# Decay attention with a softplus FFN: score halves of the later units summed out of PSUM by one reduction, masked once, then split; the low parts of k and q on VectorE

## The chip, the core and the metric

The kernel runs on one core of one Trainium2 chip. The metric is device microseconds of one execution. The median of three runs of the kernel before is 705.5 us (703.51 to 705.92).

Five engines matter here: TensorE (PE in the profile; its weight loads are listed apart as PEld), VectorE (DVE), ScalarE (ACT), GpSimd (POOL), and SyncE (SP), which issues nearly all DMAs. In this program each engine works off one queue, whose order is fixed at compile time, and semaphores tie the queues together; an instruction that waits holds up those behind it in its queue.

## The reference

```python
def _attn_ref(q, k, v):                      # (4, 8, 768, 64) each
    gamma = 1.0 - 2.0 ** (-5.0 - np.arange(H))
    scale = 1.0 / np.sqrt(D)
    state = zeros((B, H, D, D))
    for t in range(S):
        state = gamma * state + k_t (outer) v_t
        y[:, :, t] = scale * q_t @ state

def _moe_ref(x, w_in, w_out):                # x: 3072 x 512, w_in: 512 x 2048, w_out: 2048 x 512
    h = x @ w_in
    g = np.maximum(h, 0.0) + np.log1p(np.exp(-np.abs(h)))
    return g @ w_out
```

The attention's result, with heads side by side, is the x of the second function. All is float32, and the weights arrive as float64. The kernel gets its precision by splitting float32 numbers into a high part (rounded to fp32r) and a low part (the rest), and by running three matmuls for one product: high x high, high x low, low x high.

## The kernel before

**Units.** The attention runs in chunks of C = 128 tokens. A unit is one batch, one chunk and four of the eight heads (`HH = 4`, as `NJ = 2` pairs): 4 x 6 x 2 = 48 units. Every unit goes through the same parts at fixed ticks (L302: `load_unit` at -6, `decay` at -2, `operands` at 0, `scores` at 2, `new_state` at 3, `stack_and_outputs` at 5), and units follow each other every 4 ticks.

**Early and later units.** The first `WHOLE = 12` units use whole float32 matmuls. The 36 later ones use split operands:

- `load_unit` (L141) loads kn (keys by tokens, for the state), then kb and qb (keys and queries in 32-wide blocks; `load_blocks`, L131, 8 DMAs of 16 KB each, issued at L136), then vn (values by tokens), all on SP's queue. kn, kb and the pair qn/qb have two buffers each. kn is loaded for every unit, though the last chunk of a batch makes no state and never reads it. vn goes into the first of two halves of three fixed tiles `vns`; the other half is zero and serves only the early units.
- `decay` (L156) multiplies qb (L166) and vn (L167) by tables, on POOL.
- `operands` (L169): DVE transposes kb and qb in place (L185); ACT copies k's high part (L189) and q's (L192, L193); POOL subtracts for the low parts of k (L190) and of q (L194), two 64x256 instructions each. Then the split of v into `vhl` (L197 on ACT, L198 on DVE).
- `scores` (L201): for each pair j, two matmuls (L215) put into one PSUM tile `sc` two fields beside each other: field 0 is (k high and low) x q high, field 1 is that x q low. ACT copies field 0 into the high part `ah` (L217); DVE subtracts `ah` from field 0 (L218) and adds field 1 (L219), which makes `al`. After both pairs, POOL masks `ah` and `al` (L221, two instructions of 128x512).
- `new_state` (L228): the state matmuls of kn and vn (L238). `outputs` (L262): matmuls of q with the state (L287, L288), of `vhl` with `ah` and `al` (L289 to L291), then the split of the result into the ring `xh`, `xl` (L293 on ACT, L295 on DVE). `stack_state` (L246) splits the state (L258 on ACT, L260 on DVE).

**FFN.** It runs over nine blocks of tokens (`BLOCKS`: 256, 256, six of 384, 256) in steps of one or two of the sixteen 128-wide slices of `DF`. A step is `hidden` (L316, matmuls L323 to L325 out of the ring into `hp`, two PSUM buffers), `softplus_1` (L328: L330 on DVE, L331 on ACT), `softplus_2` (L333: L335 on DVE, high part gh L337 on ACT, low part gl L339 on POOL) and, two steps later, `second` (L342, L354 to L356), at whose end the results are copied out (`o`, two buffers; L366, L368) and stored (L370, on SP).

**Order.** The code spreads the ticks over the FFN's steps, so that a block's units are done about two steps ahead of it; a compile-time simulation of the engines then fixes the order on every queue. The weights (L70, L71) are loaded and converted (L78 to L99) in the first 100 us, each load paced by an earlier conversion.

Of the kernel before, what the change touches and what calls it, by code (L numbers as in the profile page):

```python
# [10 lines left out]
F32 = mybir.dt.float32  # L11
F32R = mybir.dt.float32r
# [3 lines left out]
ALU = mybir.AluOpType  # L16

P = 128
C = 128
# [6 lines left out]
WHOLE = 12  # L26
# [7 lines left out]
def decay_attention_then_softplus_ffn(ctx: ExitStack, tc: tile.TileContext, q, k, v, w_in, w_out, qtab, vtab, gtab, out):  # L34
    nc = tc.nc
    B, H, S, D = q.shape
    DM, DF = w_in.shape
    NC = S // C
# [5 lines left out]
    HH = H // 2  # L44
    NJ = HH // 2

    const = ctx.enter_context(tc.tile_pool(name="const", bufs=1))
    attn = ctx.enter_context(tc.tile_pool(name="attn", bufs=1))
# [53 lines left out]
    units = [(c // NC, c % NC, hf) for c in range(B * NC) for hf in range(2)]  # L102
    loads, live, state = {}, {}, {}
# [20 lines left out]
    vns = [attn.tile([P, HH, 2, D], F32, name=f"vn{i}") for i in range(3)]  # L124
# [4 lines left out]


    def load_blocks(nm, src, b, c, hf):  # L131
        t = attn.tile([P, NJ, C // 32, 32], F32, name=nm, tag={"qb": "qn"}.get(nm, nm), bufs=2)
        for h in range(HH):
            for d in range(0, D, 32):
                at = h % 2 * D + d
                nc.sync.dma_start(  # L136
                    t[at:at + 32, h // 2], src[b, hf * HH + h, c * C:(c + 1) * C, d:d + 32].rearrange("(i t) d -> t i d", t=32)
                )
        return t

    def load_unit(n):  # L141
        if n in loads:
            return
        b, c, hf = units[n]
        tiles = []
        for nm, src in (("kn", k), ("qn", q), ("vn", v)):
            if nm == "qn" and n >= WHOLE:
                for nm, src in (("kb", k), ("qb", q)):
                    tiles.append(load_blocks(nm, src, *units[n]))
                continue  # L150
            t = vns[n % 3][:, :, 0, :] if nm == "vn" else attn.tile([P, HH, D], F32, name=nm, bufs=2)
            nc.sync.dma_start(t, src[b, hf * HH:(hf + 1) * HH, c * C:(c + 1) * C, :].rearrange("h s d -> s h d"))
            tiles.append(t)
        loads[n] = tiles

    def decay(n):  # L156
        b, c, hf = units[n]
        vn = loads[n][-1]
        hs = slice(hf * HH, (hf + 1) * HH)
        if n < WHOLE:  # L160
            qn = loads[n][1]
            nc.gpsimd.tensor_tensor(qn, qn, qtabs[:, c, hs].unsqueeze(2).broadcast_to([P, HH, D]), op=ALU.mult)
        else:
            qb = loads[n][2].rearrange("p m i d -> p (m i) d")
            by = qblocks[:, c, hf].rearrange("p m i -> p (m i)")
            nc.gpsimd.tensor_tensor(qb, qb, by.unsqueeze(2).broadcast_to(list(qb.shape)), op=ALU.mult)  # L166
        nc.gpsimd.tensor_tensor(vn, vn, vtabs[:, c, hs].unsqueeze(2).broadcast_to([P, HH, D]), op=ALU.mult)  # L167

    def operands(n):  # L169
        b, c, hf = units[n]  # L170
        kn, *rest, vn = loads.pop(n)
        if n < WHOLE:
            tp = ps_a.tile([P, 2, NJ, C], F32, name="tp", tag="a")
            for t, x in enumerate((kn, *rest)):
                for j in range(NJ):
                    nc.tensor.transpose(tp[:, t, j, :], x[:, 2 * j:2 * j + 2, :], ident)
            qt = qs[:, n % 2]
            nc.scalar.copy(kz[lo, 0], tp[lo, 0])
            nc.vector.tensor_copy(kz[up, 1], tp[up, 0])
            nc.scalar.copy(qt, tp[:, 1])  # L180
            live[n] = [qt, kn, vn]
            return
        for x in rest:
            blocks = x.rearrange("p m i d -> p (m i d)")
            nc.vector.transpose(blocks, blocks)  # L185
        kt, qt = (x.rearrange("p m i d -> p m (i d)") for x in rest)
        kq = kqs[n % 2]
        for par, own, oth in sides:
            nc.scalar.copy(kq[own, 0, par], kt[own])  # L189
            nc.gpsimd.tensor_tensor(kq[oth, 0, par], kt[own], kq[own, 0, par].bitcast(F32), op=ALU.subtract)  # L190
        for par, own, oth in sides:
            nc.scalar.copy(kq[own, 1, par], qt[own])  # L192
            nc.scalar.copy(kq[oth, 1, par], qt[own])  # L193
            nc.gpsimd.tensor_tensor(kq[own, 2, par], qt[own], kq[own, 1, par].bitcast(F32), op=ALU.subtract)  # L194

        vhl = attn.tile([P, HH, 2, D], F32R, name="vhl", tag="vhl", bufs=2)
        nc.scalar.copy(vhl[:, :, 0, :], vn)  # L197
        nc.vector.tensor_tensor(vhl[:, :, 1, :], vn, vhl[:, :, 0, :].bitcast(F32), op=ALU.subtract)  # L198
        live[n] = [kq, vhl, kn, vn]

    def scores(n):  # L201
        kq = live[n][0]
        if n < WHOLE:
            parts = [attn.tile([P, HH, C], F32, name="ah")]
            sc = ps_a.tile([P, HH, C], F32, name="sc", tag="a")
            for h in range(HH):
                nc.tensor.matmul(sc[:, h, :], lhsT=kz[:, h % 2, h // 2, :], rhs=kq[:, h // 2, :], start=True, stop=True)
            nc.scalar.copy(parts[0], sc)
        else:
            parts = [attn.tile([P, HH, C], F32R, name=nm) for nm in ("ah", "al")]  # L210
            for j in range(NJ):

                sc = ps_a.tile([P, 2, 2, C], F32, name="sc", tag="a")
                for par in range(2):
                    nc.tensor.matmul(sc[:, par], lhsT=kq[:, 0, par, j, :], rhs=kq[:, 1:, par, j, :], start=True, stop=True)  # L215
                hi, low = (t[:, 2 * j:2 * j + 2, :] for t in parts)
                nc.scalar.copy(hi, sc[:, :, 0, :])  # L217
                nc.vector.tensor_tensor(low, sc[:, :, 0, :], hi.bitcast(F32), op=ALU.subtract)  # L218
                nc.vector.tensor_tensor(low, sc[:, :, 1, :], low.bitcast(F32), op=ALU.add)  # L219
        for t in parts:  # L220
            nc.gpsimd.affine_select(  # L221
                t, t.bitcast(F32), pattern=[[0, HH], [1, C]], compare_op=ALU.is_ge, fill=0.0, base=0, channel_multiplier=-1
            )
        live[n] += parts

    began = {}

# [72 lines left out]


    PARTS = {-6: load_unit, -2: decay, 0: operands, 2: scores, 3: new_state, 5: stack_and_outputs}  # L302
    FIRST_TICK = min(PARTS)
    PERIOD = 4
# [72 lines left out]
    for i, a, b in turns:  # L377
        m = WIDE // BLOCKS[i]
# [18 lines left out]
    for n in range(2):  # L397
        load_unit(n)
# [44 lines left out]
    for a, b in zip(starts, starts[1:]):  # L443
        i = steps[b][0]
        if i == 2:
            a = b - SPREAD
        have = ticks_for(i - 1)
        for s in range(a, b):

            t, n = (s - a + 1, b - a) if i == 2 else (min(s - a, b - a - 2), b - a - 2)  # L450
# [59 lines left out]
```

## Time and profile before

| | before |
|---|---|
| median of 3 runs | 705.5 us (703.51 to 705.92) |
| profiled execution | 702.99 us, span of its instructions 701.3 us |
| mean granted TensorE clock | 0.988 |
| PE busy | 666.4 us (95%), 4136 matmuls |
| DVE busy | 357.5 us (51%), 771 instructions |
| ACT busy | 362.5 us (52%), 844 |
| POOL busy | 387.6 us (55%), 498 |

A busy time is the union of an engine's instructions. In a list of groups, a line gives the code line, engine, operation, output and inputs, the shape and the count; behind the bar stand the total busy time in us and the mean of one in ns, and then the engine's idle time just before such instructions, with what ended it. In a timeline, the first two numbers are start and duration in us, and a bracket gives idle time before the instruction and what ended it. A stretch of the run shows its length, the busy time of PE, PEld, DVE, ACT and POOL (with instruction counts), the granted TensorE clock as a share of full speed, the share of DMA time and GB/s.

### The profile page before, as it was taken

The page shows a single profiled execution, that of the slowest core. Times are in us where ns is not written, and L with a number is a line of the kernel's source. Part 1 is how long each engine was busy: PE and PEld are TensorE (multiplying, and loading weights), DVE is VectorE, ACT ScalarE, POOL GpSimd, SP SyncE. Part 2 cuts the span into 40 slices and gives each one's busy share as a digit, 9 for nine tenths or more (in the row PEclk, how much of TensorE's full clock was granted, in tenths as well). Part 3 has the DMA queues.
Part 4 walks back from the last instruction along what each step waited for, and adds up shares of the span by engine and source line. Part 5 has one row for each costly group of instructions (what it writes and reads, how often), then busy time and mean ns, then how long its engine had stood idle before and what let it go on. Part 6 is the DMA issues. An engine that isn't in the chain of part 4 may idle for free.

```text
span 701.3 us, 13055 instructions
## 1 busy us (share of the span) xinstructions
PE 666.4 (95%) x4136; PEld 604.0 (86%) x4136; DVE 357.5 (51%) x771; ACT 362.5 (52%) x844; POOL 387.6 (55%) x498
## 2 busy tenths in 40 slices
PE   5888999999999899997999999999899999999997
PEld 4778999988999789986999979998699988999996
DVE  5757877356544554444555446444644446443321
ACT  5767776445445554454555555454555456432221
POOL 5877778545556465554655565556556556322221
PEclk9998999999999999998999999999999999999999
DMA  8889752132121331113212232121221212000100
GB/s 250 216 215 244 204 158 39 33 80 62 32 37 33 87 66 26 34 38 76 39 33 37 46 87 55 26 46 32 72 51 33 36 43 65 1 1 1 46 0 31
DMA packets 156997, 47.57 MB, mean 68 GB/s; under 512 B 143616, under 2 KB 151808, under 8 KB 156928
## 3 DMA queue, kind: packets, MB, share of 16 engines
q1 hardware_dynamic: 156480, 46.72, 28.1%
q8 instruction: 33, 0.54, 0.3%
q14 instruction: 36, 0.29, 0.1%
q10 hardware_dynamic: 448, 0.01, 0.0%
HBM read 40.39 MB, written 6.29 MB: 67 GB/s over the span
## 4 chain that ended last, share of the span: by engine, by line
PE 77%; DMA 5%; POOL 4%; ACT 3%; issue 3%; SPq 3%; DVE 2%; POOLq 0%; ACTq 0%; DVEq 0%
PE hp L323 11%; PE hp L324 11%; PE hp L325 11%; PE acc L355 11%; PE acc L354 11%; PE acc L356 11%; SPq L136 2%; PE sc L215 2%; PE stp L238 2%; DMA win<-in_moe_w_in_dram 1%; POOL kq L190 1%; PE yp L290 1%; PE yp L291 1%; PE yp L289 1%; POOL kq L194 1%
## 5 line engine op out<-in xcount | busy, mean ns | idle before, releaser
L339 POOL TENSOR_TENSOR gl<-sp,gh 128x384 fp32r<-128x384 f32 (+1 forms) x120 | 129.4, 1080 | 180.8 <-ACT gh L337 156.6
L323 PE MATMUL hp<-xh,winhl 128*128 128x384 f32 (+1 forms) x576 | 186.8, 327 | 3.4 <-ACT xh L293 1.7
L324 PE MATMUL hp<-xl,winhl 128*128 128x384 f32 (+1 forms) x576 | 185.6, 322 | 0.0
L325 PE MATMUL hp<-xh,winhl 128*128 128x384 f32 (+1 forms) x576 | 185.5, 322 | 0.0
L354 PE MATMUL acc<-wouthl,gh 128*128 128x512 f32 x384 | 152.9, 398 | 0.0
L355 PE MATMUL acc<-wouthl,gh 128*128 128x512 f32 x384 | 152.1, 396 | 0.0
L356 PE MATMUL acc<-wouthl,gl 128*128 128x512 f32 x384 | 148.5, 395 | 0.1
L331 ACT ACTIVATE sp<-sp 128x384 f32<-128x384 f32 (+1 forms) x120 | 65.5, 546 | 135.6 <-DVE sp L330 129.3
L330 DVE TENSOR_SCALAR sp<-hp 128x384 uint32<-128x384 uint32 (+1 forms) x120 | 69.4, 579 | 107.4 <-PE hp L325 103.3
L323 PEld LDWEIGHTS hp<-xh,winhl 128*128 128x128 f32 x576 | 109.4, 191 | 8.6 <-ACT xh L293 2.0
L324 PEld LDWEIGHTS hp<-xl,winhl 128*128 128x128 f32 x576 | 109.9, 191 | 3.4
L325 PEld LDWEIGHTS hp<-xh,winhl 128*128 128x128 f32 x576 | 109.7, 190 | 0.4
L337 ACT CAST gh<-sp 128x384 fp32r<-128x384 f32 (+1 forms) x120 | 64.1, 535 | 78.3 <-DVE sp L335 40.1
L335 DVE SCALAR_TENSOR_TENSOR sp<-hp,sp 128x384 f32<-128x384 f32 (+1 forms) x120 | 69.5, 579 | 42.9 <-ACT sp L331 41.7
L356 PEld LDWEIGHTS acc<-wouthl,gl 128*128 128x128 f32 x384 | 71.7, 188 | 14.8 <-POOL gl L339 0.5
L354 PEld LDWEIGHTS acc<-wouthl,gh 128*128 128x128 f32 x384 | 72.5, 189 | 11.2
L355 PEld LDWEIGHTS acc<-wouthl,gh 128*128 128x128 f32 x384 | 72.6, 189 | 11.0
L194 POOL TENSOR_TENSOR kq<-qb,kq 64x256 fp32r<-64x256 f32 x72 | 52.8, 733 | 31.9 <-ACT kq L192 24.6
L190 POOL TENSOR_TENSOR kq<-kb,kq 64x256 fp32r<-64x256 f32 x72 | 53.0, 736 | 25.4 <-ACT kq L189 20.6
L185 DVE STREAM_TRANSPOSE kb<-kb 128x256 f32<-128x256 f32 x36 | 16.0, 444 | 66.9 <-DMA kb<-in_k_dram 40.0
L192 ACT CAST kq<-qb 64x256 fp32r<-64x256 f32 x72 | 29.0, 403 | 33.2 <-PE yp L287 26.7
L295 DVE TENSOR_TENSOR xl<-yp,xh 64x256 fp32r<-64x256 f32 x72 | 30.0, 417 | 22.7 <-ACT xh L293 21.8
(80 smaller groups left out, 1010.5 us busy)
## 6 DMA issues: line engine op xcount, KB each, us to landing
win<-in_moe_w_in_dram SPq DMA_DIRECT2D x16, 512.0 KB, 4.5
wout<-in_moe_w_out_dram SPq DMA_DIRECT2D x16, 512.0 KB, 4.2
kn<-in_k_dram SPq DMA_DIRECT2D x48, 128.0 KB, 2.3
vn<-in_v_dram SPq DMA_DIRECT2D x48, 128.0 KB, 2.6
out_dram<-o SPq DMA_DIRECT2D x24, 256.0 KB, 2.1
kb<-in_k_dram SPq DMA_DIRECT2D x288, 16.0 KB, 1.7
qb<-in_q_dram SPq DMA_DIRECT2D x288, 16.0 KB, 1.7
qn<-in_q_dram SPq DMA_DIRECT2D x12, 128.0 KB, 3.3
```

Of the source, the lines that this page charges most:

```text
L190: nc.gpsimd.tensor_tensor(kq[oth, 0, par], kt[own], kq[own, 0, par].bitcast(F32), op=ALU.subtract)
L323: nc.tensor.matmul(hp[:, k], lhsT=wt[:, 0, d, :], rhs=xh[:, d, :], start=d == 0, stop=False)
L324: nc.tensor.matmul(hp[:, k], lhsT=wt[:, 0, d, :], rhs=xl[:, d, :], start=False, stop=False)
L325: nc.tensor.matmul(hp[:, k], lhsT=wt[:, 1, d, :], rhs=xh[:, d, :], start=False, stop=d == ND - 1)
L330: nc.vector.tensor_scalar(sp.bitcast(U32), hps[s].bitcast(U32), 0x80000000, None, op0=ALU.bitwise_or)
L331: nc.scalar.activation(sp, sp, AF.Softplus)
L335: nc.vector.scalar_tensor_tensor(g, hps.pop(s), 0.0, g, op0=ALU.max, op1=ALU.add)
L337: nc.scalar.copy(gh, g)
L339: nc.gpsimd.tensor_tensor(gl, sps.pop(s), gh.bitcast(F32), op=ALU.subtract)
L354: nc.tensor.matmul(acc[i][t], lhsT=gh[:, k, ts], rhs=wt[:, 0], start=begins and k == 0, stop=False)
L355: nc.tensor.matmul(acc[i][t], lhsT=gh[:, k, ts], rhs=wt[:, 1], start=False, stop=False)
L356: nc.tensor.matmul(acc[i][t], lhsT=gl[:, k, ts], rhs=wt[:, 0], start=False, stop=ends and f == fs[-1])
```

## The change

For the later units only:

- **Scores.** The ACT copy out of PSUM and the two DVE instructions per pair (L217 to L219) go. One DVE `tensor_reduce` per pair adds the two fields straight out of PSUM into a new float32 tile `a`. POOL masks `a` once instead of `ah` and `al`. Only then ACT copies `a` into `ah` (one instruction, 128x512), and POOL subtracts (`al = a - ah`, one instruction, 128x512).
- **Low parts.** The four subtractions per unit for the low parts of k and q move from POOL to DVE.
- **Loads.** kb and qb now share the two buffers of kn and qn, so kb's own tiles are gone. Keys by tokens go into the second half of the `vns` tile, behind kb and qb in SP's queue, and are not loaded for the last chunk of a batch.

```diff
     def load_blocks(nm, src, b, c, hf):
-        t = attn.tile([P, NJ, C // 32, 32], F32, name=nm, tag={"qb": "qn"}.get(nm, nm), bufs=2)
+        t = attn.tile([P, NJ, C // 32, 32], F32, name=f"{nm[0]}b", tag=nm, bufs=2)
...
+    def tokens_of(n):
+        t = vns[n % 3]
+        if n < WHOLE:
+            return t[:, :, 0, :], None
+        t = t.rearrange("p h t d -> p (h t d)").rearrange("p (t h d) -> p t h d", t=2, h=HH)
+        return t[:, 0], t[:, 1]
...
+        vn, kn = tokens_of(n)
+        if n < WHOLE:
+            tiles = [by_tokens(attn.tile([P, HH, D], F32, name=nm, bufs=2), src) for nm, src in (("kn", k), ("qn", q))]
+        else:
+            tiles = [load_blocks(nm, src, b, c, hf) for nm, src in (("kn", k), ("qn", q))]
+            if c < NC - 1:
+                by_tokens(kn, k)
+        tiles.append(by_tokens(vn, v))
         loads[n] = tiles
...
             nc.scalar.copy(kq[own, 0, par], kt[own])
-            nc.gpsimd.tensor_tensor(kq[oth, 0, par], kt[own], kq[own, 0, par].bitcast(F32), op=ALU.subtract)
+            nc.vector.tensor_tensor(kq[oth, 0, par], kt[own], kq[own, 0, par].bitcast(F32), op=ALU.subtract)
...
-            nc.gpsimd.tensor_tensor(kq[own, 2, par], qt[own], kq[own, 1, par].bitcast(F32), op=ALU.subtract)
+            nc.vector.tensor_tensor(kq[own, 2, par], qt[own], kq[own, 1, par].bitcast(F32), op=ALU.subtract)
...
-                hi, low = (t[:, 2 * j:2 * j + 2, :] for t in parts)
-                nc.scalar.copy(hi, sc[:, :, 0, :])
-                nc.vector.tensor_tensor(low, sc[:, :, 0, :], hi.bitcast(F32), op=ALU.subtract)
-                nc.vector.tensor_tensor(low, sc[:, :, 1, :], low.bitcast(F32), op=ALU.add)
-        for t in parts:
-            nc.gpsimd.affine_select(
-                t, t.bitcast(F32), pattern=[[0, HH], [1, C]], compare_op=ALU.is_ge, fill=0.0, base=0, channel_multiplier=-1
-            )
-        live[n] += parts
+                nc.vector.tensor_reduce(a[:, 2 * j:2 * j + 2, :], sc.rearrange("p h t c -> p h c t"), axis=mybir.AxisListType.X, op=ALU.add)
+        nc.gpsimd.affine_select(a, a, pattern=[[0, HH], [1, C]], compare_op=ALU.is_ge, fill=0.0, base=0, channel_multiplier=-1)
+        live[n].append(a)
+        if n >= WHOLE:
+            ah, al = (attn.tile([P, HH, C], F32R, name=nm) for nm in ("ah", "al"))
+            nc.scalar.copy(ah, a)
+            nc.gpsimd.tensor_tensor(al, a, ah.bitcast(F32), op=ALU.subtract)
+            live[n][-1:] = [ah, al]
```

More of the change, by code (lines that the diff above doesn't have):

```diff
@@ L144, in load_unit, with by_tokens @@
         b, c, hf = units[n]
[L145 to L151, printed above, removed]
-            nc.sync.dma_start(t, src[b, hf * HH:(hf + 1) * HH, c * C:(c + 1) * C, :].rearrange("h s d -> s h d"))
-            tiles.append(t)
+        def by_tokens(t, src):
+            nc.sync.dma_start(t, src[b, hf * HH:(hf + 1) * HH, c * C:(c + 1) * C, :].rearrange("h s d -> s h d"))
+            return t
+        vn, kn = tokens_of(n)
[6 more added lines that the diff above has]
+        tiles.append(by_tokens(vn, v))
         loads[n] = tiles
@@ L163, in decay @@
         else:
-            qb = loads[n][2].rearrange("p m i d -> p (m i) d")
+            qb = loads[n][1].rearrange("p m i d -> p (m i) d")
             by = qblocks[:, c, hf].rearrange("p m i -> p (m i)")
@@ L170, in operands @@
         b, c, hf = units[n]
-        kn, *rest, vn = loads.pop(n)
+        *rest, vn = loads.pop(n)
         if n < WHOLE:
             tp = ps_a.tile([P, 2, NJ, C], F32, name="tp", tag="a")
-            for t, x in enumerate((kn, *rest)):
+            for t, x in enumerate(rest):
                 for j in range(NJ):
@@ L180, in operands @@
             nc.scalar.copy(qt, tp[:, 1])
-            live[n] = [qt, kn, vn]
+            live[n] = [qt, rest[0], vn]
             return
@@ L198, in operands @@
         nc.vector.tensor_tensor(vhl[:, :, 1, :], vn, vhl[:, :, 0, :].bitcast(F32), op=ALU.subtract)
-        live[n] = [kq, vhl, kn, vn]
+        live[n] = [kq, vhl, tokens_of(n)[1], vn]
     def scores(n):
         kq = live[n][0]
+        a = attn.tile([P, HH, C], F32, name="a")
         if n < WHOLE:
-            parts = [attn.tile([P, HH, C], F32, name="ah")]
             sc = ps_a.tile([P, HH, C], F32, name="sc", tag="a")
@@ L207, in scores @@
                 nc.tensor.matmul(sc[:, h, :], lhsT=kz[:, h % 2, h // 2, :], rhs=kq[:, h // 2, :], start=True, stop=True)
-            nc.scalar.copy(parts[0], sc)
+            nc.scalar.copy(a, sc)
         else:
-            parts = [attn.tile([P, HH, C], F32R, name=nm) for nm in ("ah", "al")]
             for j in range(NJ):
```

## The prediction, made before the changed kernel was run

> **What bounds the kernel now.** I read the view of stretches first, by stage of the kernel. Each row has the stretch, its length, then the busy time of PE, PEld, DVE, ACT and POOL, the granted TensorE clock, the DMA share and GB/s.
>
> ```profile
> 0.00:40.00 40.00, 28.21 (x191) 24.57 (x192) 26.55 (x59) 26.99 (x55) 26.27 (x46) 1.00 0.88 236
> 40.00:60.00 20.00, 17.08 (x103) 15.89 (x103) 13.34 (x24) 15.00 (x33) 16.65 (x23) 0.83 0.86 227
> 100.00:160.00 60.00, 60.00 (x405) 55.24 (x404) 34.43 (x69) 31.82 (x73) 37.28 (x44) 1.00 0.26 62
> 160.00:600.00 440.00, 424.92 (x2577) 384.31 (x2576) 220.34 (x511) 230.64 (x570) 252.28 (x334) 0.99 0.23 47
> ```
>
> PE is the bound: it is busy without a gap from 100 to 160 us, and 424.9 of 440 us while the later units run. No matmul is added or removed, so the change can only move time in which PE waits or runs at a lower clock. Between 160 and 600 us the waits are 440 - 424.92 = 15.1 us. DVE, ACT and POOL are each busy 50 to 57% of that stage, so none of them is a bound by its sum; what counts is where a queue is late.
>
> The view of waits, PE's own, says for what (total us, times, longest):
>
> ```profile
> PE yp L289 <- POOL ah L221: 4.4, 3, 3.0
> PE stp L238 <- DVE st L260: 3.7, 3, 2.6
> PE stp L238 <- ACT stw L254: 2.9, 1, 2.9
> PE yp L290 <- POOL al L221: 2.5, 4, 0.9
> ```
>
> Two of the four largest end with POOL's masks L221. The timeline places them near 241, 325 and 490 us, where a new FFN block needs the last units of its tokens; the L254 wait lies at 54 us. After three waits the granted clock is halved for a while, and those stretches read:
>
> ```profile
> 51.00:59.50 8.50, 5.58 (x25) 5.47 (x25) 7.12 (x14) 7.79 (x18) 6.80 (x8) 0.63 1.06 284
> 324.00:333.00 9.00, 6.37 (x27) 5.54 (x28) 3.65 (x9) 2.98 (x8) 4.19 (x8) 0.63 0.25 52
> 239.50:244.00 4.50, 2.78 (x11) 2.79 (x12) 3.52 (x9) 3.04 (x9) 0.91 (x2) 0.67 0.45 125
> ```
>
> The work lost to the clock is about (1 - clock) x PE's busy time: 0.37 x 5.58 = 2.1 us, 0.37 x 6.37 = 2.4 us, 0.33 x 2.78 = 0.9 us. Waits and lost clock together are what the change can win back in the stage of the later units: 15.1 + 2.4 + 0.9 = 18.4 us. The same sum is what it can make larger.
>
> **The price of each instruction.** From the list of groups with shapes kept apart (behind the bar: total us, mean ns):
>
> ```profile
> L190 POOL TENSOR_TENSOR kq<-kb,kq 64x256 fp32r<-64x256 f32 x72 | 53.0, 736 | 25.4 <-ACT kq L189 20.6
> L218 DVE TENSOR_TENSOR al<-sc,ah 128x256 fp32r<-128x256 f32 x72 | 30.3, 420 | 16.7 <-ACT ah L217 15.7
> L219 DVE TENSOR_TENSOR al<-sc,al 128x256 fp32r<-128x256 f32 x72 | 29.7, 412 | 0.8
> L217 ACT CAST ah<-sc 128x256 fp32r<-128x256 f32 x72 | 26.4, 367 | 4.1 <-PE sc L215 3.3
> L221 POOL TENSOR_SCALAR_AFFINE_SELECT al<-al 128x512 fp32r<-128x512 f32 x36 | 22.9, 635 | 0.4
> L99 POOL TENSOR_TENSOR winhl<-w,winhl 128x512 fp32r<-128x512 f32 x16 | 20.6, 1290 | 6.4 <-ACT winhl L98 6.3
> L198 DVE TENSOR_TENSOR vhl<-vn,vhl 128x256 fp32r<-128x256 f32 x36 | 16.5, 459 | 0.1
> L335 DVE SCALAR_TENSOR_TENSOR sp<-hp,sp 128x512 f32<-128x512 f32 x24 | 16.5, 689 | 11.6 <-ACT sp L331 11.4
> L98 ACT CAST winhl<-w 128x512 fp32r<-128x512 f32 x16 | 9.9, 618 | 1.3 <-DVE w L96 1.1
> ```
>
> The new reduction has no row. It reads 512 elements a partition out of PSUM and writes 256: at the least the 0.42 us of L218 (256 elements), at the most two such passes and half again, 1.29 us like L99. I take L335's 0.69 us, a DVE instruction that reads 512 elements from PSUM. A low part on DVE has no row either; nearest is L198, two SBUF operands of 256 elements, 0.46 us in the mean. The new subtraction on POOL is L99's form (1.29 us) and the new copy on ACT is L98's (0.62 us).
>
> Per later unit, then. **DVE**: minus 2 x (0.42 + 0.41), plus 2 x 0.69, plus 4 x 0.46 = +1.56 us, over 36 units +56 us: 357 becomes 413 us, 59% of the span. **POOL**: minus 4 x 0.74, minus one mask 0.635, plus 1.29 = -2.3 us, or -83 us: 388 becomes 305 us, 43%. **ACT**: minus 2 x 0.37, plus 0.62 = -0.1 us. All of this lies beside PE's work and changes the time only through the waits, taken one by one.
>
> **The boundary at 325 us.** The timeline of POOL, and the PE instruction that it releases (start, duration):
>
> ```profile
> 320.51 0.62 POOL L166 TENSOR_TENSOR qb<-qb,qblocks 128x256 f32<-128x256 f32 x1 [4.12 <-DMA qb<-in_q_dram]
> 321.20 0.73 POOL L190 TENSOR_TENSOR kq<-kb,kq 64x256 fp32r<-64x256 f32 x1
> 322.00 0.71 POOL L194 TENSOR_TENSOR kq<-qb,kq 64x256 fp32r<-64x256 f32 x1
> 322.69 0.60 POOL L167 TENSOR_TENSOR vn<-vn,vtabs 128x256 f32<-128x256 f32 x1
> ...
> 325.68 0.63 POOL L221 TENSOR_SCALAR_AFFINE_SELECT al<-al 128x512 fp32r<-128x512 f32 x1
> 326.37 0.37 PE L290 MATMUL yp<-al,vhl 128*64 128x128 f32 x1 [0.95 <-POOL al L221]
> ```
>
> From qb's landing to the last mask POOL works off L166, L167, four low parts and two masks: 0.62 + 0.60 + 4 x 0.73 + 2 x 0.63 = 5.4 us, and PE stands behind them. In the new queue it is L166, L167, one mask, then ACT's copy 0.62 and the subtraction 1.29: 3.8 us. So PE starts about 1.6 us earlier. Of the 2.4 us that the clock takes here I count half, 1.2 us, since a shorter wait may or may not still halve it. Term: **-2.8 us**. The boundary at 490 us has the same sequence with one more instruction ahead of the low parts; the same 1.6 us comes out, without the clock. Term: **-1.6 us**.
>
> **The boundary at 241 us.** Here another chain ends last:
>
> ```profile
> 234.16 1.54 POOL L190 TENSOR_TENSOR kq<-kb,kq 64x256 fp32r<-64x256 f32 x2
> 239.85 0.69 DVE L368 COPY o<-acc 128x512 f32<-128x512 f32 x1 [3.15 <-DMA out_dram<-o]
> 241.22 1.23 PE L238 MATMUL stp<-vn,kn 128*128 128x128 f32 x4 [2.55 <-DVE st L260]
> ```
>
> POOL's L190 pair releases kb's buffer; SP, which holds the next kb loads back for it, has a store of `o` queued behind them; DVE waits for that store before L368, and L260 stands behind L368. With the low parts on DVE, directly behind ACT's copies, the buffer comes free without POOL's queue: about the pair's 1.5 us earlier. Term: **-1.5 us**. The other boundaries wait less than 1 us for one thing each and I count them at nothing. At all six, DVE's 1.56 us more per unit and the longer split behind the mask (below) can show; I count **+1 us** for the stage.
>
> **The start.** kb has buffers of its own now, so its loads for the first four later units are issued in the middle of the weights' loads. In the new kernel they share kn's buffers, which the early units hold until the state matmuls of units 10 and 11; they move behind 80 us, where SP has room and PE no gap. The rows (issues within 35 to 70 us, then the two waits):
>
> ```profile
> L136 SPq DMA_DIRECT2D kb<-in_k_dram x32: 371/432/1229, 36.0 to 68.2; - x32
> 51.51 0.45 DVE L185 STREAM_TRANSPOSE kb<-kb 128x256 f32<-128x256 f32 x1 [3.25 <-DMA kb<-in_k_dram]
> 53.94 1.22 PE L238 MATMUL stp<-vn,kn 128*128 128x128 f32 x4 [2.92 <-ACT stw L254]
> ```
>
> 32 issues x 0.43 = 14 us of SP's queue leave this stretch, and with them four transposes on DVE. One of those blocked DVE for 3.25 us just ahead of the weight conversion and the state copies that PE's 2.92 us wait hangs on. At stake are 2.9 + 2.1 (clock) = 5.0 us. A weight load is also part of that chain and stays (DMA share 0.86 in 40 to 60 us), so I take **-3 us**, with ends at 0 and -6 us. The 16 KB loads cost the same wherever they stand; six kn loads of the last chunks fall away, hidden before and after.
>
> **Sum**: -3 - 1.5 - 2.8 - 1.6 + 1 = -7.9 us, or -8. The profiled execution took 702.99 us, 2.5 us below the median of the runs shown, 705.5. The waits are those of the profiled one, the forecast is made against the median: **697.5 us**.
>
> **Rivals.**
>
> *Slower: the split behind the mask.* Before, from masked input to the last operand takes two masks, 2 x 0.635 = 1.27 us; after, mask, ACT copy and POOL subtraction, 0.635 + 0.62 + 1.29 = 2.55 us, through two more queue changes. Ahead of the mask, 0.37 + 0.42 + 0.41 becomes 0.69, which leaves +0.8 us per unit. ACT's copy also waits for POOL now: where POOL stands before L166 for a DMA (4.12 us above) with the mask behind it, ACT and its softplus stand too. It decides where POOL's low parts are not what made the wait; then PE's wait grows by 0.8 us at each unit without slack. At all 36 that would be 29 us; with one unit in three it is 12 x 0.8 = 9.6 us, less the start's 3: about +6.5 us, **712 us**. For it: the L289 and L290 waits show that this chain is the tight one. Against: two of the three boundaries show low parts in that very queue.
>
> *DVE and POOL in each other's way.* The trace has it:
>
> ```profile
> 184.36 1.02 POOL L339 TENSOR_TENSOR gl<-sp,gh 128x384 fp32r<-128x384 f32 x1 [2.26 <-ACT gh L337]
> 184.41 1.25 DVE L198 TENSOR_TENSOR vhl<-vn,vhl 128x256 fp32r<-128x256 f32 x1
> ```
>
> L198 lasts until 0.28 us after POOL's end, 0.79 us over its mean. It is the only such instruction per later unit now; four more join it, and POOL gains a long subtraction. If a third of the 144 lose 0.79 us, DVE loses 38 us, nearly all in idle time; at six boundaries it would cost 0.8 us each, +5 us, so **702.5 us**. The Trainium skill's page SBUF — State Buffer, "Who interferes with whom", says that a VectorE instruction with two SBUF inputs and a GpSimd instruction that reads SBUF exclude each other, the second waiting for the first's end; this row agrees. By that rule the reduction, with one input, is exempt.
>
> *No change.* The planner's new order puts as many gaps elsewhere: **705.5 us**.
>
> *More than forecast.* All boundary gaps close and the clock holds: -5 at the start, 8 to 15 us behind it: about **688 us**.
>
> **The numbers.** The forecast (690 to 701.5 us) gets 0.41, more than that 0.09, the DVE-POOL rival 0.12 (half of it within 0.3%), no change 0.10, slower 0.28. About 0.3%, 2.1 us, is what a measurement of this kernel can tell from no change. Faster: 0.41 + 0.09 + 0.06 = 0.56; within: 0.10 + 0.06 = 0.16; slower: 0.28. The range reaches from 685 us to 712.5 us; below lie 0.05 and above some 0.12.
>
> **What would show it.** Right: POOL near 305 us and DVE near 415 us busy; reductions near 0.69 us; no kb load before 80 us and no wait for L254 near 54 us; waits for L289 and L290 shorter, the clock above 0.988. Wrong: PE waits that end with the new subtraction or ACT's copy (the split), low parts at 0.8 us or more on DVE (the port), a reduction near 1.3 us, or new waits at boundaries that are tight now by less than 1 us, since the order on every queue is drawn up anew.

## The result, and the profile after

| | before, run beside it | after |
|---|---|---|
| median of 4 runs | 704.5 us (702.37 to 705.92) | 686.42 us (683.91 to 688.11) |
| ratio to before, 95% interval | | 0.9743 (0.9697 to 0.9789) |
| profiled execution | 702.99 us, span 701.3 us | 688.11 us, span 686.0 us |
| mean granted clock | 0.988 | 0.992 |

The change makes the kernel 2.6% faster, about 18 us by the medians, where 8 us was forecast. The direction was right; the size is more than double, and the time after stands just above the lower end of the range.

The page of the changed kernel gives each engine's busy time, share of the span and instructions:

```profile
PE 661.4 (96%) x4136; PEld 601.1 (88%) x4136; DVE 433.2 (63%) x843; ACT 357.2 (52%) x808; POOL 315.0 (46%) x354
```

The span is 15.3 us shorter. PE's idle time fell from 701.3 - 666.4 = 34.9 to 686.0 - 661.4 = 24.6 us, which is 10.3 us of it; the other 5.0 us are in PE's busy time, with the same 4136 matmuls. The view of stretches says where (columns as in the prediction):

```profile
0.00:40.00 40.00, 29.93 (x192) 26.60 (x193) 26.22 (x59) 27.09 (x55) 26.32 (x45) 0.96 0.89 237
40.00:60.00 20.00, 19.99 (x145) 18.50 (x144) 14.86 (x25) 16.34 (x35) 17.87 (x23) 1.00 0.90 261
0.00:100.00 100.00, 87.61 (x604) 80.15 (x605) 72.56 (x140) 72.73 (x148) 69.19 (x92) 0.98 0.80 219
100.00:160.00 60.00, 56.81 (x372) 51.06 (x370) 44.32 (x78) 31.77 (x69) 31.87 (x33) 1.00 0.28 61
160.00:600.00 440.00, 435.27 (x2666) 396.07 (x2667) 292.40 (x588) 231.77 (x554) 193.43 (x213) 0.99 0.22 45
...
18.00:25.00 7.00, 4.68 (x26) 4.25 (x26) 5.22 (x10) 4.54 (x10) 4.95 (x6) 0.76 0.96 245
158.00:165.00 7.00, 5.00 (x33) 4.80 (x32) 5.71 (x14) 4.88 (x13) 2.85 (x3) 0.76 0.34 97
540.00:548.00 8.00, 6.73 (x27) 6.17 (x28) 7.56 (x15) 4.37 (x12) 3.04 (x3) 0.79 0.11 16
```

The first 100 us of the kernel before, in the same view:

```profile
0.00:100.00 100.00, 83.84 (x566) 76.15 (x567) 70.75 (x135) 71.38 (x145) 72.46 (x97) 0.97 0.81 220
```

In the first 60 us PE works 4.6 us more than before (1.7 in the first stretch, 2.9 in the second), and the clock between 40 and 60 us is 1.00 where it was 0.83; over the first 100 us its idle time falls from 16.2 to 12.4 us. From 100 to 160 us PE loses 3.2 us where it lost nothing. From 160 to 600 us its idle time falls from 15.1 to 4.7 us. That last step, 10.4 us, is the bulk of the gain, and the forecast had 4.9 us there, 1.2 us of it for the clock.

PE's own waits, with what ended them (total us, times, longest):

```profile
PE sc L223 <- DVE a L224: 4.1, 4, 1.9
PE tp L186 <- DMA kn<-in_k_dram: 3.6, 1, 3.6
PE yp L297 <- POOL al L230: 2.0, 1, 2.0
PE tp L186 <- DVE wp L95: 1.9, 1, 1.9
...
PE yp L296 <- ACT ah L229: 0.7, 2, 0.4
```

L223 is the scores matmul and L224 the new reduction, L296 and L297 the output matmuls with `ah` and `al`, L229 and L230 the new split, L225 the one mask; L186 belongs to the early units. The state waits (L238 before) are gone. What is left of the wait for the masked operands is 2.0 + 0.7 us, against 4.4 + 2.5.

The groups that the prediction priced, with shapes kept apart:

```profile
L224 DVE TENSOR_REDUCE a<-sc 128x256 f32<-128x512 f32 x72 | 48.8, 679 | 7.1 <-PE sc L223 4.1 <-POOL al L230 2.5
L230 POOL TENSOR_TENSOR al<-a,ah 128x512 fp32r<-128x512 f32 x36 | 47.8, 1327 | 9.3 <-ACT ah L229 9.1
L200 DVE TENSOR_TENSOR kq<-kb,kq 64x256 fp32r<-64x256 f32 x72 | 45.3, 629 | 3.2 <-ACT kq L199 1.0
L225 POOL TENSOR_SCALAR_AFFINE_SELECT a<-a 128x512 f32<-128x512 f32 x48 | 35.1, 730 | 43.2 <-DVE a L224 39.3 <-ACT a L218 2.3 <-ACT kq L199 1.2
L204 DVE TENSOR_TENSOR kq<-qb,kq 64x256 fp32r<-64x256 f32 x72 | 34.9, 485 | 5.1 <-ACT kq L202 4.0
```

The reduction takes 0.68 us (0.69 was taken), the subtraction on POOL 1.33 (1.29), q's low parts 0.49 and k's 0.63 us (0.46 for both). Nothing in these prices explains a gain twice as large.

### The profile page after: what moved, and what is told of

It reads as the page before. It is cut to its first block, busy times and chain, and to the rows that moved or that the text cites. A ratio compares the mean times of both kernels' runs of the same rounds, so it can differ in the third digit from the quotient of the medians.

```text
span 686.0 us, 12848 instructions
## 1 busy us (share of the span) xinstructions
PE 661.4 (96%) x4136; PEld 601.1 (88%) x4136; DVE 433.2 (63%) x843; ACT 357.2 (52%) x808; POOL 315.0 (46%) x354
## 4 chain that ended last, share of the span: by engine, by line
PE 70%; SPq 8%; DMA 8%; DVE 5%; issue 4%; ACT 3%; POOL 2%; POOLq 0%; DVEq 0%; ACTq 0%
PE hp L330 10%; PE hp L332 10%; PE hp L331 10%; PE acc L361 10%; PE acc L363 10%; PE acc L362 10%; SPq L136 7%; DMA win<-in_moe_w_in_dram 2%; DMA vn<-in_v_dram 2%; PE sc L223 2%; PE stp L245 2%; DMA qb<-in_q_dram 1%; DVE kq L200 1%; PE yp L296 1%; PE yp L297 1%
## 5 line engine op out<-in xcount | busy, mean ns | idle before, releaser
L346 POOL TENSOR_TENSOR gl<-sp,gh 128x384 fp32r<-128x384 f32 (+1 forms) x120 | 130.8, 1090 | 227.8 <-ACT gh L344 198.9
L363 PE MATMUL acc<-wouthl,gl 128*128 128x512 f32 x384 | 150.7, 396 | 0.1
L342 DVE SCALAR_TENSOR_TENSOR sp<-hp,sp 128x384 f32<-128x384 f32 (+1 forms) x120 | 69.5, 579 | 35.8 <-ACT sp L338 34.9
L225 POOL TENSOR_SCALAR_AFFINE_SELECT a<-a 128x512 f32<-128x512 f32 x48 | 35.1, 730 | 43.2 <-DVE a L224 39.3
L224 DVE TENSOR_REDUCE a<-sc 128x256 f32<-128x512 f32 x72 | 48.8, 679 | 7.1 <-PE sc L223 4.1
L230 POOL TENSOR_TENSOR al<-a,ah 128x512 fp32r<-128x512 f32 x36 | 47.8, 1327 | 9.3 <-ACT ah L229 9.1
L200 DVE TENSOR_TENSOR kq<-kb,kq 64x256 fp32r<-64x256 f32 x72 | 45.3, 629 | 3.2 <-ACT kq L199 1.0
L195 DVE STREAM_TRANSPOSE kb<-kb 128x256 f32<-128x256 f32 x36 | 16.0, 445 | 49.3 <-DMA kb<-in_k_dram 37.9
```

The costliest lines, as they stand in the source:

```text
L200: nc.vector.tensor_tensor(kq[oth, 0, par], kt[own], kq[own, 0, par].bitcast(F32), op=ALU.subtract)
L342: nc.vector.scalar_tensor_tensor(g, hps.pop(s), 0.0, g, op0=ALU.max, op1=ALU.add)
L346: nc.gpsimd.tensor_tensor(gl, sps.pop(s), gh.bitcast(F32), op=ALU.subtract)
L363: nc.tensor.matmul(acc[i][t], lhsT=gl[:, k, ts], rhs=wt[:, 0], start=False, stop=ends and f == fs[-1])
```

## The experiments

The change has three parts that can be taken apart: the scores (reduction, one mask, split behind it), the low parts on DVE, and the loads. The scores without the loads weren't tried: the new tile `a` takes the room that kb's tiles had.

Each ratio below is to the kernel before, run beside the kernel on the same chip; differences in us are differences of ratios times 703 us. The changed kernel with its low parts left on GpSimd ran twice, at 0.9626 and 0.9605; differences against it are taken from the first, so they carry some 1.5 us of doubt, unless another kernel is named. "Idle" is PE's idle time from 160 to 600 us, that is 440 less PE's busy time in the row of that stretch.

### Which part wins

Two theories stood at the start. By the prediction, POOL's queue makes the waits, and taking the low parts out of it is what wins. By the rival, the scores win: before, `ah` and `al` have one buffer each and are written straight out of PSUM, so nothing of unit n+1's scores can leave PSUM before unit n's last output matmul has read them. The new tile `a` stands between.

**Low parts alone.** Before, with this edit:

```diff
-            nc.gpsimd.tensor_tensor(kq[oth, 0, par], kt[own], kq[own, 0, par].bitcast(F32), op=ALU.subtract)
+            nc.vector.tensor_tensor(kq[oth, 0, par], kt[own], kq[own, 0, par].bitcast(F32), op=ALU.subtract)
...
-            nc.gpsimd.tensor_tensor(kq[own, 2, par], qt[own], kq[own, 1, par].bitcast(F32), op=ALU.subtract)
+            nc.vector.tensor_tensor(kq[own, 2, par], qt[own], kq[own, 1, par].bitcast(F32), op=ALU.subtract)
```

> The kernel before with one edit: the low parts of k and q (four 64x256 subtractions per later unit) on VectorE; scores and loads as before. Theory POOL queue (PE waited at block boundaries because GpSimd's queue was late by the four low parts, 2.9 us per unit): most of the 13 to 16 us gained behind 160 us is here, 690 to 694 us, GpSimd near 283 us busy and VectorE near 430. Rival score path (one mask, the reduction and the tile a made the gain): little changes or VectorE gets late, 702 to 708 us. Rival loads: 704 us.

Measured: 722.89 us, ratio 1.0282 (1.0239 to 1.0326), some 20 us slower. The stretch, and four of PE's waits in it:

```profile
160.00:600.00 440.00, 415.98 (x2483) 373.19 (x2482) 272.27 (x614) 218.49 (x547) 162.05 (x200) 0.98 0.22 46
...
PE hp L323 <- ACT xh L293: 5.4, 3, 2.6
PE sc L215 <- DVE al L219: 4.7, 6, 1.9
...
PE yp L289 <- POOL ah L221: 3.5, 5, 1.0
PE yp L290 <- POOL al L221: 2.0, 6, 0.5
```

Idle rises to 24.0 us. POOL's work in this stretch falls from 252 to 162 us, and PE's waits for POOL's two masks fall with it, but only from 6.9 to 5.5 us (the longest from 3.0 to 1.0 us), in 11 places instead of 7. Other waits more than take their place: 5.4 us for the result `xh` (1.7 before) and 4.7 us for DVE's `al` (1.0 before). A shorter queue on POOL doesn't win time by itself here. DVE's queue is longer in this kernel, so this run alone doesn't say how much of the new waits is DVE's load.

**Loads alone.** Before, with the functions `load_blocks`, `tokens_of`, `load_unit` and the lines of `decay` and `operands` that read the tiles, as in the change's diff.

> The kernel before with one edit: kb and qb in the buffers of kn and qn, keys by tokens in the second half of vns and behind kb and qb on SP's queue, none for a batch's last chunk. Theory POOL queue: the boundary waits stay, only the start changes (5 us earlier at 100 us, given back by 160 us as in the changed kernel), 701 to 705 us. Rival loads (the three-deep keys and the order on SP's queue bring the units in time): 690 to 694 us. Score path: 704 us.

Measured: 706.06 us, ratio 1.0043 (1.0022 to 1.0064).

```profile
0.00:100.00 100.00, 86.71 (x591) 79.30 (x592) 70.35 (x134) 72.62 (x148) 71.89 (x97) 0.97 0.79 219
160.00:600.00 440.00, 421.44 (x2543) 381.43 (x2542) 219.92 (x505) 227.01 (x564) 248.75 (x330) 0.98 0.21 44
...
PE yp L299 <- POOL ah L231: 5.7, 3, 2.9
...
PE yp L300 <- POOL al L231: 1.9, 3, 0.9
```

The first 100 us lose 13.3 us of PE's time; before they lost 16.2. So the loads bring the forecast 3 us at the start by themselves. They give it back later: idle is 18.6 instead of 15.1 us. The last two lines are PE's waits for the masks (L231 here).

**Without the low parts.** After, with the two subtractions back on POOL (the diff above, reversed).

> The changed kernel with the low parts of k and q back on GpSimd; scores and loads as changed. Theory POOL queue: GpSimd near 407 us busy (the new subtraction is there too), the boundary waits come back, 698 to 706 us. Rival score path: keeps the gain, 686 to 691 us.

Measured: 675.93 us, ratio 0.9626 (0.9577 to 0.9676): faster than the whole change. The stretch, and two groups:

```profile
160.00:600.00 440.00, 439.85 (x2712) 401.28 (x2711) 230.28 (x464) 232.48 (x554) 279.38 (x338) 1.00 0.21 44
...
L225 POOL TENSOR_SCALAR_AFFINE_SELECT a<-a 128x512 f32<-128x512 f32 x48 | 30.5, 636 | 18.8 <-DVE a L224 11.8 <-ACT a L218 3.6 <-ACT kq L202 1.4
L208 DVE TENSOR_TENSOR vhl<-vn,vhl 128x256 fp32r<-128x256 f32 x36 | 24.2, 672 | 1.0
```

PE is idle for 0.15 us in 440, at full clock, with POOL's queue fuller (279 us) than before (252 us). Against the loads alone, the scores are worth 0.0417, or 29 us.

**Without the scores.** After, with `scores` as before.

> The changed kernel with the scores as before (ScalarE copy, two VectorE instructions, two masks); low parts on VectorE and loads as changed. Theory POOL queue: most of the gain stays, 687 to 692 us, VectorE near 440 us busy. Rival score path: the boundary waits come back, 698 to 706 us.

Measured: 708.95 us, ratio 1.0082 (1.0055 to 1.0109), idle 18.8 us. Of PE's waits in the stretch:

```profile
PE hp L333 <- ACT xh L303: 5.4, 3, 2.6
...
PE yp L299 <- POOL ah L231: 1.1, 2, 0.9
PE yp L300 <- POOL al L231: 0.6, 3, 0.2
```

The gain is gone. All four agree: the scores win it, and the low parts on DVE cost. This kernel differs from the loads alone by the low parts only. Taking those out of POOL's queue cuts the waits for the masks from 7.6 to 1.7 us, and PE's idle time doesn't move (18.6 and 18.8 us), since the waits for `xh` grow from 1.7 to 5.4 us and those for DVE's `al` from 0.3 to 5.0 us.

What the low parts on DVE cost depends on what stands around them: 20 us with the loads and the scores of before, 3 us with the new loads (1.0082 against 1.0043), 8 us with the new loads and scores. Why the loads of before make them so dear was not tried.

### What in the scores wins

Three kernels start from the best one so far, the changed kernel without the low parts ("the base" from here on).

**The tie put back.** The base, with each later unit's reductions made to wait for the last output matmul of the unit before:

```diff
-                nc.vector.tensor_reduce(a[:, 2 * j:2 * j + 2, :], ...)
+                r = nc.vector.tensor_reduce(a[:, 2 * j:2 * j + 2, :], ...)
+                if n - 1 in spent:
+                    tc.add_manual_dep(r.ins, spent[n - 1].name, ...)
...
-                nc.tensor.matmul(o, lhsT=vhl[:, h, 1, :], rhs=ah[:, h, :], start=False, stop=True)
+                m = nc.tensor.matmul(o, lhsT=vhl[:, h, 1, :], rhs=ah[:, h, :], start=False, stop=True)
+        spent[n] = m.ins
```

> The kernel with the scores and loads as changed and the low parts on GpSimd (675.9 us), plus one wait: each later unit's reductions wait for the last output matmul of the unit before it, as the first score instruction had to before the change, when ah and al (one buffer each) were written straight out of PSUM. Theory untied units (the gain of the scores part is that a unit's sums and mask run ahead of the outputs of the unit before): most of the boundary waits come back, 692 to 703 us. Rivals (PSUM is freed sooner by one reduction; one mask instead of two): no change, 675 to 679 us.

Measured: 710.16 us, ratio 1.0099 (1.0066 to 1.0132): 33 us slower than the base, slower than the kernel before. The stretch and PE's waits in it:

```profile
160.00:600.00 440.00, 421.40 (x2531) 381.88 (x2530) 214.25 (x443) 222.14 (x533) 268.65 (x329) 0.97 0.22 44
...
PE yp L299 <- POOL al L232: 6.5, 5, 1.7
PE hp L333 <- ACT xh L303: 4.7, 5, 1.2
PE sc L223 <- DVE a L224: 2.6, 3, 0.9
PE yp L298 <- ACT ah L231: 2.0, 3, 0.9
```

The reduction, the single mask and the new split are all there; only their freedom to run ahead is gone, and with it the whole gain. What comes late is the end of the unit's chain: the operands `ah` and `al`, and the result `xh` that the FFN reads.

The tie can be seen at the boundary near 327 us of the kernel before (timeline: start, duration):

```profile
324.96 0.46 PE L215 MATMUL sc<-kq 128*128 128x256 f32 x2
...
327.49 0.31 PE L291 MATMUL yp<-ah,vhl 128*64 128x128 f32 x1
327.84 0.74 ACT L293 CAST xh<-yp 64x256 fp32r<-64x256 f32 x2 [5.16 <-PE yp L291]
328.60 0.37 ACT L217 CAST ah<-sc 128x256 fp32r<-128x256 f32 x1
```

The next unit's first scores are in PSUM by 325.4 us. ACT does nothing for 5.16 us until the last output matmul, and only behind the result's copy, at 328.60 us, does it read them. A stretch of the base's timeline near 300 us has it the other way round:

```profile
299.87 0.67 DVE L224 TENSOR_REDUCE a<-sc 128x256 f32<-128x512 f32 x1
...
301.01 0.22 PE L298 MATMUL yp<-ah,vhl 128*64 128x128 f32 x1
301.27 0.74 ACT L300 CAST xh<-yp 64x256 fp32r<-64x256 f32 x2 [0.77 <-PE yp L298]
```

Over the whole run this can be counted: for the 35 pairs of successive later units, the start of the first instruction that reads unit n+1's scores, less the start of unit n's last output matmul, both from the timeline.

| kernel | reads ahead, of 35 pairs | median |
|---|---|---|
| before | 0 | +2.8 us |
| loads alone; low parts alone; without the scores | 0 | +2.8 to +2.9 us |
| base, tie put back | 0 | +0.3 us |
| after | 12 | +1.1 us |
| base | 23 | -0.8 us |

**The reduction as two instructions.** The base, with ACT's copy of field 0 into `a` and DVE's addition of field 1:

```diff
-                nc.vector.tensor_reduce(a[:, 2 * j:2 * j + 2, :], ...)
+                aj = a[:, 2 * j:2 * j + 2, :]
+                nc.scalar.copy(aj, sc[:, :, 0, :])
+                nc.vector.tensor_tensor(aj, sc[:, :, 1, :], aj, op=ALU.add)
```

> The 675.9 us kernel with the reduction taken apart: per pair ScalarE copies field 0 into a and VectorE adds field 1 from PSUM, the rest as there. PSUM's score tile is held 0.8 us and through two queues instead of 0.68 us and one. Theory untied units: 675 to 681 us. Rival PSUM freed sooner: half of the gain or more goes, 688 us or over.

Measured: 680.25 us, ratio 0.9672 (0.9643 to 0.97), idle 1.1 us. The single reduction is worth 3 to 5 us, little clear of the noise; 26 of the 35 pairs still read ahead.

**The split ahead of two masks.** The base, with the mask moved behind the split and applied to both halves, as before:

```diff
-        nc.gpsimd.affine_select(a, a, ...)
+        if n < WHOLE:
+            mask(a)
...
             nc.gpsimd.tensor_tensor(al, a, ah.bitcast(F32), op=ALU.subtract)
+            mask(ah)
+            mask(al)
```

> The 675.9 us kernel with the split ahead of the masks: a is copied and subtracted unmasked, and GpSimd masks ah and al apart, two masks of 0.64 us instead of one. Theory untied units: 675 to 681 us, GpSimd near 435 us busy. Rival one mask: the boundary waits come back, 688 us or over.

Measured: 684.43 us, ratio 0.9717 (0.9682 to 0.9753), idle 5.7 us, 27 of 35 pairs ahead. The single mask ahead of the split is worth 6 to 8 us. Both are small beside the 33 us of the tie.

### What the low parts on DVE cost

The whole change against the base is 0.9743 to 0.9626: 8 us. Three explanations were open: DVE is simply loaded with more instructions; two-input instructions on DVE and POOL's stand in each other's way; or kb and qb are held longer, so that their loads come later.

**Four more instructions with one input.** The base, with four unused reductions per unit on DVE, reading q's and k's high parts.

```diff
+        for par, own, oth in sides:
+            for hi in (kq[own, 0, par], kq[own, 1, par]):
+                scr = attn.tile([P, NJ, C // 2], F32, name="scr")
+                nc.vector.tensor_reduce(scr[own], hi.bitcast(F32).rearrange("p j (c t) -> p j c t", t=2), axis=mybir.AxisListType.X, op=ALU.add)
```

> The 675.9 us kernel with four extra VectorE reductions per later unit (64x256 in, one SBUF input, result not used), placed where the low parts of k and q stand in the changed kernel and each waiting for the ScalarE copy of a high part; the low parts stay on GpSimd. It gives VectorE's queue the low parts' load without their second SBUF input and without k's and q's buffers hanging on it. If the 10.5 us that the low parts cost on VectorE are its queue's load: 684 to 690 us. If they are the waits of VectorE and GpSimd for each other, or the buffers: 676 to 680 us.

Measured: 681.44 us, ratio 0.9688 (0.9658 to 0.9718), idle 2.5 us.

**Four more with two inputs from SBUF.** The same place, with subtractions of two high parts:

```diff
+            for x, y in (2 * ((kq[own, 0, par].bitcast(F32), kq[own, 1, par]),)):
+                scr = attn.tile([P, NJ, C], mybir.dt.bfloat16, name="scr")
+                nc.vector.tensor_tensor(scr[own], x, y.bitcast(F32), op=ALU.subtract)
```

> As the run with four extra one-input reductions per later unit (681.4 us against 675.9 without), but each extra VectorE instruction is a subtraction with two SBUF inputs (64x256 in, two high parts of k and q, result not used), as the low parts are. If VectorE's and GpSimd's waits for each other are the other half of the low parts' price: 684 to 689 us and instructions of over 0.6 us among the extra ones. If not: 680 to 683 us.

Measured: 684.85 us, ratio 0.9725 (0.9699 to 0.975), idle 5.1 us. The group's row in the one-input kernel, then in the two-input kernel:

```profile
L209 DVE TENSOR_REDUCE scr<-kq 64x128 f32<-64x256 f32 x144 | 58.9, 409 | 13.1 <-ACT kq L202 10.0
```

```profile
L209 DVE TENSOR_TENSOR scr<-kq 64x256 bf16<-64x256 f32 x144 | 89.4, 621 | 12.2 <-ACT kq L202 9.3
```

**The same, holding the blocks.** Two inputs as well, but kb and qb are read, as the real low parts do:

```diff
+            for x, y in ((kt[own], kq[own, 0, par]), (qt[own], kq[own, 1, par])):
```

> The same four extra subtractions, but reading k's and q's transposed blocks, so that these buffers come free for the next loads only behind VectorE's queue as well, as in the changed kernel; GpSimd still makes the low parts. If the buffers' hold is the missing part: 685 to 692 us where the run with two high parts stays near 681. If it is not: within 2 us of that run.

Measured: 683.66 us, ratio 0.9719 (0.9697 to 0.9742), idle 4.0 us: the same as without holding them.

**Order alone.** To see what a mere change of the compile-time order does: the base, with v's split written ahead of the low parts in `operands`.

> The 675.9 us kernel with v's split written ahead of k's and q's in the code: the same instructions and buffers, only another order for the planner. It shows how much a new order alone moves the time. If the scores part, not a lucky order, makes the gain: 673 to 681 us. If the order makes it: anything up to 700 us.

Measured: 675.97 us, ratio 0.9605 (0.9583 to 0.9627): no change against the base with this one other order. The last three kernels ran on one chip, so this one serves the two before it for comparison.

So four more DVE instructions per unit whose output nobody reads cost 4 to 6 us with one input (from 0.9626 and from 0.9605) and 8 us with two (from 0.9605), which is about the low parts' own price. That load on DVE costs is shown against 0.9605, whose interval lies clear of the one-input kernel's. That the second input costs on top is suggested by 621 against 409 ns each, but the two ratios' intervals overlap. Holding the blocks plays no part.

**k's low parts alone on DVE**, and **q's alone**: the base with one of the two lines changed.

> The 675.9 us kernel with only k's low parts on VectorE and q's on GpSimd. If each low part on VectorE costs the same: 680 to 682 us. If k's cost most (their mean is 0.63 us there, q's 0.49): 683 to 687 us. If VectorE takes two per unit in its idle time: 675 to 678 us.

> The 675.9 us kernel with only q's low parts on VectorE and k's on GpSimd, the mirror of the run with k's alone (676.2 us). If q's place in the chain makes the price (q comes last of a unit's loads, and its low parts stand in VectorE's queue in front of the reductions): 683 to 688 us. If it is the number of instructions, two being free and four not: 675 to 678 us.

> The 675.9 us kernel once more, beside the run above on the same chip, for a closer interval and as the version to carry: 674 to 679 us.

The last is the base once more, beside q's. Measured: k's 676.2 us, ratio 0.9612 (0.9578 to 0.9646), idle 0.2 us; q's 680.69 us, 0.9702 (0.9677 to 0.9727), idle 1.9 us; the base 674.75 us, 0.9605 (0.9588 to 0.9622), idle 0.3 us. k's cost nothing, q's 0.0097 or 7 us. Why q's and not k's was not tried further: no run separates their cost from their place in DVE's queue.

**The best version** is the base: the scores and the loads of the change, the low parts left on GpSimd. At 0.9605 to 0.9626 it beats both kernels.

## Why the prediction was right in direction and wrong in size

**The bound: right.** PE stayed the bound, no matmul was added, and the time came out of its waits: idle time from 160 to 600 us went from 15.1 to 4.7 us, and over the run by 10.3 us. The work lost to the half clock fell only from 5.4 us to 0.24 x 4.68 + 0.24 x 5.00 + 0.21 x 6.73 = 3.7 us, since new stretches took the place of the old. That leaves some 3 us of PE's shorter busy time unplaced.

**The prices: right, but for k's low parts and POOL's mask.** Reduction, copy on ACT and subtraction on POOL came within 3%. DVE is busy 433 us, not 413, and POOL 315, not 305. DVE's 20 us are k's low parts, 72 x (0.63 - 0.46) = 12 us, q's, 2 us, and L208, the split of v, which takes 0.66 us in the changed kernel, 36 x (0.66 - 0.46) = 7 us. POOL's 10 us are its mask, 48 x (0.730 - 0.635) = 5 us, the subtraction, 1 us, and small rises in its other groups. So the mechanism of the DVE-POOL rival is there (its rows are in the section on the hardware), and the low parts do cost; the time that this rival gave, 702.5 us, didn't come, because the scores win more than three times as much.

**The start, -3 us: right where it was counted, but no gain over the run.** PE's idle time in the first 100 us fell from 16.2 to 12.4 us; the loads alone do 2.9 of it. There is no wait for L254 near 54 us any more. The first kb load is issued at 77.9 us, 2 us sooner than the 80 us that were named:

```profile
L136 SPq DMA_DIRECT2D kb<-in_k_dram x288: 311/430/1594, 77.9 to 552.5; - x144
```

What the prediction had not counted is what the loads part costs later, 3.5 us of idle time when it stands alone: over the whole run the loads alone are 0.4% slower than before.

**The boundaries at 241, 325 and 490 us, -5.9 us: the step that failed.** The prediction read in POOL's queue which instructions stand ahead of the last mask, saw four low parts there (and at 241 the same low parts holding kb's buffer), and counted the time that they take as time that PE wins. The reading of the queue holds. Near 325 us, in the kernel before (ACT, then POOL):

```profile
320.60 0.36 ACT L217 CAST ah<-sc 128x256 fp32r<-128x256 f32 x1
324.16 0.63 POOL L221 TENSOR_SCALAR_AFFINE_SELECT ah<-ah 128x512 fp32r<-128x512 f32 x1
```

`ah` is whole at 320.96 us and its mask starts 3.2 us later, behind POOL's other work. The step from there to PE's time failed. With the low parts out of POOL's queue PE's waits for the masks do shrink, and its idle time doesn't (18.6 to 18.8 us with the new loads, 15.1 to 24.0 us with the old): PE then waits for `xh` and for DVE. The mask was not the only late part of the unit. Near 325 us its first scores left PSUM at 317.50 us, directly behind the copy of the unit before's result, while POOL stood idle for 4.12 us up to 320.51 us; up to 316.7 us the unit before held `ah` and `al`. The base, with all four low parts on POOL, is idle for 0.15 us, so they needn't leave it. That the sign came out right is luck as far as this term goes: the part that it rests on is slower by itself (1.0282). The cure was another part of the same diff, which the prediction priced as an exchange of instructions (a reduction for three, a mask less, a longer split) and not as a new buffer. Putting the tie back costs 33 us, the whole gain. Whether the tie was the last thing waited for at each single unit is not shown: before, the next unit's scores are read 2.8 us behind the output matmul in the median, not at once, and in the tied kernel 0.3 us. The order on the queues is drawn up around the tie, and that order and the tie can't be told apart here. Nor was the most direct trial made, two buffers for `ah` and `al` in the kernel before.

**The rival "more than forecast", 688 us: nearest in time, with a chance of 0.09.** It had all boundary gaps closing and the clock holding. Most of the gaps closed, 4.7 us of idle time from 160 to 600 us are left, and the clock still fell in three stretches; it named no cause, so the hit is of the number only.

**The slower rival (the split behind the mask): didn't appear.** It has 2.7 us of PE's waits left. The chain behind the mask is longer, as worked out, but with `a` in front of it units can start earlier, which 12 pairs of 35 do in the changed kernel.

**The +1 us for DVE's load: much too small.** The low parts cost 8 us. One of PE's remaining waits shows how a queue that isn't full can hold up PE. Of the changed kernel's timeline:

```profile
540.20 0.45 DVE L195 STREAM_TRANSPOSE kb<-kb 128x256 f32<-128x256 f32 x1 [2.45 <-DMA kb<-in_k_dram]
540.57 0.65 DVE L224 TENSOR_REDUCE a<-sc 128x256 f32<-128x512 f32 x1
...
541.27 0.51 PE L223 MATMUL sc<-kq 128*128 128x256 f32 x2 [1.71 <-DVE a L224]
```

DVE is at the head of its queue with a transpose whose load hasn't landed, and waits 2.45 us. The reduction is behind it, and PE needs the PSUM buffer that the reduction frees. An in-order engine waits for one load, and PE waits for that engine. In the base PE has no such wait, though DVE's transposes of kb wait for its loads longer there (53.4 us in all, 37.9 here). That the low parts make the difference at this place is not shown.

## What to carry to other kernels

Where an in-order engine stands at a late unit, ask first what that unit's *first* instruction waits for, not which instructions stand ahead of its last one: a tile with one buffer, written early and read late, ties each unit to the end of the one before, and putting that tie back cost 33 us here. A gap that ends with one late instruction needn't close when that instruction comes sooner: see whether others of the same unit are late as well. Work isn't free on an engine that is half idle; four short instructions per unit, their results unused, cost 4 to 8 us on a VectorE that was busy for about half of the run. A change of several parts is best run by its parts: here one part won 29 us, and another gave 8 of them back.

## What the runs showed of the hardware

**DVE and POOL lengthen each other.** A pair of k's low parts in the changed kernel, beside POOL (timeline):

```profile
371.19 1.01 POOL L346 TENSOR_TENSOR gl<-sp,gh 128x384 fp32r<-128x384 f32 x1 [3.76 <-ACT gh L344]
371.39 1.84 DVE L200 TENSOR_TENSOR kq<-kb,kq 64x256 fp32r<-64x256 f32 x2 [0.34 <-ACT kq L199]
372.15 0.80 POOL L176 TENSOR_TENSOR qb<-qb,qblocks 128x256 f32<-128x256 f32 x1
372.91 0.82 POOL L225 TENSOR_SCALAR_AFFINE_SELECT a<-a 128x512 f32<-128x512 f32 x1
```

The pair takes 1.84 us, where the shortest single one of them takes 0.42 us; POOL's next two take 0.80 and 0.82 us, where L176's form took 0.62 us (L166 in the prediction's timeline) and L225 takes 0.64 us in the base. That POOL is lengthened as well was not expected: over the whole run its mask takes 730 ns with the low parts on DVE and 636 without. The Trainium skill's page SBUF — State Buffer, "Who interferes with whom", says that a VectorE instruction with two SBUF inputs and a GpSimd instruction that reads SBUF contend. The trace agrees so far as both engines' instructions take longer. The two kernels with unused instructions show the second input's part: with one input each of them takes 0.37 to 0.42 us and POOL's mask 638 ns, with two they take 0.37 to 1.40 us and the mask 672. L208, the split of v on DVE, takes 672 ns in the base too, against 459 before, so there the low parts are not the cause. Nor is POOL's new long subtraction alone: the tied kernel has it as well, and there L208 takes 430 ns. What stands beside the split in the untied order was not looked into.

**Short waits can halve the clock.** In the changed kernel PE's waits of 2.00 us (at 160.36) and 1.71 us (at 541.27) lie in the two stretches above with a granted clock of 0.76 and 0.79; after a wait of 1.86 us at 379.89 the clock stayed at 1.00 from 378 to 386 us. A narrower stretch shows the half:

```profile
160.30:163.50 3.20, 3.14 (x21) 3.14 (x22) 2.33 (x6) 2.01 (x7) 1.01 (x2) 0.50 0.46 133
```

In the kernel with two masks a longer wait, 2.51 us at 319.51, left the clock at 1.00 (316 to 326 us). The work lost in the two stretches is 1.2 and 1.4 us, so such a wait can cost 1.6 to 1.8 times its size; which one does can't be told from its length.
